# Two spectral and two dense layers on one core: rows loaded in quarters, one step of an order moved, fewer products with zeros at the seams

## The chip, the cores and the metric

The kernel runs on one core of a Trainium2 chip. The metric is the device time of one execution, in microseconds (us); lower is better. The profile is one execution of the same program, recorded instruction by instruction; its times count from the first instruction.

## The reference

The input x is a matrix of S = 2048 tokens by D = 1024 features, in bf16. Four layers follow one another, each with a residual and a layer norm in front of it:

```python
x = x + A(layernorm(x), A_w_r, A_w_i)      # spectral
x = x + B(layernorm(x), B_w1, B_b1, B_w2)  # dense
x = x + A(layernorm(x), A_w_r, A_w_i)
x = x + B(layernorm(x), B_w1, B_b1, B_w2)
```

A is a filter in the frequency domain: a real two-dimensional FFT over tokens and features, a product with the complex filter w_r + i w_i (2048 by 513), and the inverse transform. B is a feed-forward block: h = x w1 + b1 with 3584 hidden features, the activation Mish(h) = h tanh(softplus(h)), and a product with w2 back to 1024 features. A and B have the same weights in both of their layers.

## The kernel before

**Scheduling.** All instructions are written out in Python in one fixed order for each engine: TensorE (PE), VectorE (DVE), ScalarE (ACT), GpSimd (POOL) and SyncE (SP, which only issues DMAs here). Waits on semaphores are derived from which buffers an instruction reads and writes. There is no planner: the order in the text is the order on each engine. A DMA is issued by SP, ACT or POOL, in that engine's order, and the first two each have a queue of their own.

**Spectral layer (layer_A).** The FFTs are products with tables of sines and cosines.

- `s1` (L619 to L647) transforms along the outer token index. It consists of 16 groups j of eight products of 128 columns (L634). The stationary operand is the row buffer XR, in which the token rows are laid out as 128 partitions by 128 positions n by 128 features; group j reads the positions 8j to 8j+7. In layer 0 the moving operand is a table `MN`, the transform's table multiplied with each token's layer-norm scale, made group by group in `scaled` (ACT at L609 for group 1; POOL at L615 for 2, 4, 9, 10, 11 and 13; DVE at L615 for the others). Each group's result is copied out of PSUM by ACT (L640) or DVE (L642). In layer 1 the rows are already normalised and MN isn't needed. Eight PSUM banks make four pairs; one group fills one pair. In layer 0, s1 has three of them, because a fourth holds the scales.
- `s2` (L741) is the transform along features, `s3` (L786 to L789) the inner transform along tokens, followed by the product with the filter on DVE (L800 to L807); `i1` (L842) and `i2` (L872, L904) are the inverses. These four run over eight groups g with two halves each, in an order that is written out by hand in `order_A` (L1009): each number is stage, group and half, with 2 for s2, 3 for s3, 4 for i1 and 5 for i2. So 221 is the second half of s2 for group 2, and 400 the first half of i1 for group 0. Every step takes the next pair of banks in turn. The result of an s2 step is copied by ACT (L776) or DVE (L778), of s3 by ACT (L798), of i1 by ACT (L858) and of i2 by ACT (L916) or DVE (L914).
- In layer 0, `filter_bins` (L1032 to L1048) brings the filter into the order of the transform beside this, with four small products, two copies on DVE (L1043) and two on ACT (L1047) for each group.
- `u_turn` writes each group's result of i2 to a scratch tensor in HBM and reads it back with tokens and features exchanged. For the last group, ACT writes it in two halves, and four reads follow, two from ACT's queue and two from SP's (`u_last`, L948).

**The start (prologue).** SP issues, in this order: x in twelve pieces (a thirteenth comes from ACT), two small tables, the rows XR from x in packets of 256 bytes, then the tables FD and JT, the filter's rows for the first two groups, and more tables. A group of s1 waits for the part of the rows that it reads (`self.r_xr[j // 4]`).

**The seam between a spectral and a dense layer.** After the last step of order_A, TensorE has nothing real to do until the last group has been written to HBM and read back. In the text it goes on like this (L996 to L998):

```python
        self.spin(4, 0)
        self.residual_first()
        self.hold(11 if li else 16, 7)
```

`spin` makes four products of 512 columns whose result isn't used. `residual_first` puts the residual of the first 512 tokens into all eight banks. `hold` (L656) adds products with a stationary operand of zeros to bank 7, where they change nothing; they keep TensorE busy. Then the dense layer starts with `i4` (L1071), the last inverse transform. Its first 32 products wait for the first of the four reads; two more products with zeros and the next 32 follow. Its results are copied by `out_first` (L1082), normalised and turned, and the first products of the dense layer (L1220) follow.

**Dense layer (layer_B).** Products with w1 (L1220, L1260) and w2 (L1359), arranged with sums and differences of blocks so that seven block products do the work of eight. It isn't touched by the change.

Of the kernel before, what the change touches and what calls it, by code (L numbers as in the profile page):

```python
# [180 lines left out]
class KB:  # L181
# [200 lines left out]
    def prologue(self):  # L382
        sp = self.sp
        self.op(self.pool, lambda e: e.memset(self.EPS[:], 1e-5), writes=[self.r_eps, self.r_warm])
        xt = self.x[0].rearrange("(t p) d -> p t d", p=P)

        for a, b in ((10, 11), (0, 1), (1, 2), (11, 12), (2, 3), (3, 4), (12, 13), (4, 6), (13, 14), (6, 8), (14, 15), (8, 10), (15, 16)):
            self.dma(self.act if a == 10 else sp, self.XS[:, a:b, :], xt[:, a:b, :], f"x{a}", writes=self.r_xs[a:b])
        self.warm(ACT.Sqrt)
        small = {}  # L390
        def load_small(name, n, d):
            b = self.alloc(name, self.o[name], [n], d)
            self.dma(sp, b.ap, self.con[name], name.lower(), writes=[b.res])
            small[name] = b
        load_small("M0", P, BF)
        load_small("IDF", P, F32)
        self.M0, self.IDF = small["M0"], small["IDF"]

        self.XR = self.alloc("XR", self.o["XR"], [P, P])
        self.r_xr = []  # L400
        xv = self.x[0].rearrange("(n2 n1) (h l) -> h n2 n1 l", n2=16, l=P)
        for q, n in ((0, 2), (2, 1), (3, 1)):
            r = Res(f"xr{q}")
            for h in range(8):
                s = slice(32 * q, 32 * (q + n))
                self.dma(sp, self.XR.ap[h:P:8, s, :], xv[h][:, s, :], f"xr{q}", parts=[r])
            self.r_xr += [r] * n
        self.dma(sp, self.FD[:], self.con["FD"], "fd", writes=[self.r_fd])
        load_small("JT", 4 * P, BF)
        self.JT, self.r_jt = small["JT"].ap, small["JT"].res  # L410
        self.w1_next = 0
# [299 lines left out]
    def layer_A(self, li):  # L711
# [283 lines left out]
                u_turn(g, h)  # L995
        self.spin(4, 0)  # L996
        self.residual_first()
        self.hold(11 if li else 16, 7)  # L998
        if li == 0:
            self.op(self.pool, lambda e: e.tensor_copy(self.B1[:], self.B1h[:]), reads=[self.r_b1h], writes=[self.r_b1])  # L1000
        self.w1_buf = [self.alloc(f"W1_{i}", (self.ob["WS"] + i * 4096, 140 * K)[i > 4], [8, 256]) for i in range(4 if li else 6)]
# [3 lines left out]
    @staticmethod  # L1005
    def order_A():


        order = ("200 201 210 211 300 301 220 310 400 221 311 401 230 320 410 500 231 321 411 501 330 331 420 510 240 511 421 241 "  # L1009
                 "250 251 340 341 520 350 430 260 521 431 440 261 351 441 530 531 360 361 270 450 451 271 540 541 550 551 460 370 "  # L1010
                 "461 371 560 561 470 471 570 571")
        return [tuple(map(int, w)) for w in order.split()]
# [800 lines left out]
```

## Time and profile before

| | |
|---|---|
| Time, median of 3 runs | 928.98 us (928.76 to 930.48) |
| Span of the profiled execution | 923.2 us |
| TensorE busy | 877.7 us, 95% |
| DVE, ACT, POOL busy | 623.4, 435.0, 147.7 us |
| Granted TensorE clock, mean | 1.000 |
| Spectral layer 0, from the first product of s1 to the last of i2 | 24.0 to 102.2 us |
| Spectral layer 1, the same | 481.1 to 550.7 us |
| Products with zeros (L656), both seams | 31, of 379 ns each by the profile |

Matmuls are pipelined: the profile gives 379 ns to one of 512 columns, but such products start 0.216 us apart. So the time that a run of them takes is read from their starts. In the timeline a line is start, duration, engine, line of the kernel, operation, out<-in and count; in brackets stands the idle time of the engine before it and what ended it. In the chain of work that ended last, each piece is start, duration and the engine and line that held the end back.

### The profile page before, as it was taken

The page shows a single profiled execution, that of the slowest core. Times are in us where ns is not written, and L with a number is a line of the kernel's source. Part 1 is how long each engine was busy: PE and PEld are TensorE (multiplying, and loading weights), DVE is VectorE, ACT ScalarE, POOL GpSimd, SP SyncE. Part 2 cuts the span into 40 slices and gives each one's busy share as a digit, 9 for nine tenths or more (in the row PEclk, how much of TensorE's full clock was granted, in tenths as well). Part 3 has the DMA queues.
Part 4 walks back from the last instruction along what each step waited for, and adds up shares of the span by engine and source line. Part 5 has one row for each costly group of instructions (what it writes and reads, how often), then busy time and mean ns, then how long its engine had stood idle before and what let it go on. Part 6 is the DMA issues. An engine that isn't in the chain of part 4 may idle for free.

```text
span 923.2 us, 13610 instructions
## 1 busy us (share of the span) xinstructions
PE 877.7 (95%) x5503; PEld 471.1 (51%) x5503; DVE 623.4 (68%) x995; ACT 435.0 (47%) x645; POOL 147.7 (16%) x170
## 2 busy tenths in 40 slices
PE   0899889999999999999998998999999999999998
PEld 0677576444444444444456766754444444444443
DVE  7798468686889667568767765676747655554463
ACT  7898485456203485420018966757540025552000
POOL 0732004960004651010121200000000000000000
PEclk9999999999999999999999999999999999999999
DMA  9979861575786388364723786345166645732432
GB/s 279 284 249 287 219 194 67 210 266 139 262 281 239 131 317 298 121 233 143 281 92 114 221 217 161 137 175 184 23 197 189 204 148 180 269 121 86 173 129 102
DMA packets 153502, 175.98 MB, mean 191 GB/s; under 512 B 75000, under 2 KB 132568, under 8 KB 153320
## 3 DMA queue, kind: packets, MB, share of 16 engines
q1 hardware_dynamic: 140256, 130.32, 45.9%
q0 software_dynamic: 10032, 42.90, 12.5%
q10 hardware_dynamic: 3152, 1.90, 0.7%
q8 instruction: 43, 0.70, 0.3%
q14 instruction: 19, 0.16, 0.0%
HBM read 130.78 MB, written 40.89 MB: 186 GB/s over the span
## 4 chain that ended last, share of the span: by engine, by line
PE 88%; DVE 6%; ACT 3%; SPq 2%; DMA 1%; issue 0%; DVEq 0%
PE PS L1359 37%; PE PS L1260 30%; PE PS L1220 6%; PE PS L741 3%; PE PS L842 2%; PE PS L872 2%; SPq L251 2%; PE PS L1071 2%; PE PS L634 1%; PE PS L651 1%; ACT ARENA L640 1%; PE PS L1181 1%; PE PS L904 1%; PE PS L1060 1%; ACT ARENA L451 1%; PE PS L656 1%
## 5 line engine op out<-in xcount | busy, mean ns | idle before, releaser
L1359 PE MATMUL PS<-ARENA 128*128 128x512 bf16 x1568 | 340.1, 379 | 0.0
L1260 PE MATMUL PS<-ARENA 128*128 128x512 bf16 (+1 forms) x1288 | 280.4, 379 | 0.8 <-DVE ARENA L1265 0.8
L1359 PEld LDWEIGHTS PS<-ARENA 128*128 128x128 bf16 x1568 | 153.3, 98 | 184.5
L1265 DVE TENSOR_TENSOR ARENA<-PS,ARENA 128x512 f32<-128x512 f32 x230 | 157.1, 691 | 100.2 <-PE PS L1260 92.4
L1260 PEld LDWEIGHTS PS<-ARENA 128*128 128x128 bf16 x1288 | 125.3, 98 | 153.3 <-DVE ARENA L1265 3.6
L1270 ACT ACTIVATE ARENA<-ARENA,B 128x512 bf16<-128x512 f32 x138 | 98.8, 721 | 69.1 <-DVE ARENA L1265 63.8
L573 ACT ACTIVATE ARENA<-PS 128x512 f32<-128x512 f32 (+3 forms) x86 | 61.6, 726 | 110.6 <-PE PS L1260 92.5
L1153 POOL TENSOR_TENSOR ARENA<-ARENA 128x512 bf16<-128x512 bf16 x56 | 71.5, 1278 | 74.3 <-DVE ARENA L522 61.1
L451 ACT ACTIVATE ARENA<-XS 128x1024 bf16<-128x1024 bf16 x60 | 63.2, 1053 | 36.6 <-DVE XS L1410 33.0
L1220 PE MATMUL PS<-ARENA 128*128 128x256 bf16 (+1 forms) x528 | 73.4, 295 | 3.4 <-DVE ARENA L1186 1.9
L1384 DVE TENSOR_TENSOR ARENA<-ARENA 128x3584 bf16<-128x3584 bf16 x32 | 63.9, 2017 | 0.0
L1410 DVE TENSOR_TENSOR XS<-PS,ARENA 128x512 bf16<-128x512 f32 x52 | 35.7, 689 | 39.0 <-PE PS L1359 38.7
L1220 PEld LDWEIGHTS PS<-ARENA 128*128 128x128 bf16 x528 | 50.3, 98 | 22.3 <-DVE ARENA L1186 3.3
L1402 DVE TENSOR_TENSOR ARENA<-PS,ARENA 128x512 f32<-128x512 f32 x48 | 32.9, 688 | 28.0 <-PE PS L1359 27.6
L1224 ACT ACTIVATE ARENA<-PS,B 128x256 bf16<-128x256 f32 (+1 forms) x66 | 33.0, 515 | 29.0 <-PE PS L1220 28.8
L1270 ACT ACTIVATE ARENA<-PS,B 128x512 bf16<-128x512 f32 x46 | 31.5, 685 | 18.4 <-PE PS L1260 18.4
L1398 DVE TENSOR_TENSOR ARENA<-ARENA,XS 128x512 f32<-128x512 f32 x52 | 36.8, 731 | 0.5
L442 ACT ACTIVATE RS<-MV,EPS 128x1 f32<-128x1 f32 (+2 forms) x11 | 3.3, 296 | 71.5 <-DVE MV L564 70.1
L741 PE MATMUL PS<-FD,ARENA 128*128 128x256 bf16 (+1 forms) x256 | 31.4, 271 | 2.5 <-ACT ARENA L640 2.5
L842 PE MATMUL PS<-ARENA 128*128 128x256 bf16 x256 | 32.6, 273 | 1.0 <-DVE ARENA L807 0.6
L798 ACT ACTIVATE ARENA<-PS 128x1024 bf16<-128x1024 f32 x30 | 30.4, 1046 | 5.0 <-PE PS L789 5.0
L1235 DVE TENSOR_TENSOR ARENA<-ARENA 128x2048 f16<-128x2048 bf16 x16 | 25.3, 1583 | 9.0 <-PE PS L1220 8.7
(102 smaller groups left out, 811.4 us busy)
## 6 DMA issues: line engine op xcount, KB each, us to landing
ARENA<-in_B_w_dram SPq DMA_DIRECT2D x30, 896.0 KB, 6.7
ARENA<-w1s_scratch SPq DMA_DIRECT2D x28, 896.0 KB, 4.7
ARENA<-w2s_scratch SPq DMA_DIRECT2D x24, 896.0 KB, 6.6
w1s_scratch<-ARENA POOLq DMA_DIRECT2D x14, 896.0 KB, 4.6
ARENA<-in_B_w_dram SPq DMA_DIRECT2D x24, 512.0 KB, 4.3
u_scratch<-ARENA SPq DMA_DIRECT2D x14, 512.0 KB, 4.9
ARENA<-u_scratch SPq DMA_DIRECT2D x14, 512.0 KB, 6.0
w2s_scratch<-ARENA POOLq DMA_DIRECT2D x8, 896.0 KB, 4.1
```

Of the source, the lines that this page charges most:

```text
L451: self.op(act, lambda e, i=i, f=f: e.activation(junk.ap, x, f, accum_out=sums[:, i:i + 1]), reads=[self.r_xs[j]], writes=[junk.res], parts ...
L573: fn = (lambda e: e.activation(dst, src, ACT.Copy)) if scale is None else \
L741: fns.append(lambda e: e.matmul(dst, at(r), FD[:, t:t + n], start=start, stop=stop))
L842: fns.append(lambda e, c=c, part=part: e.matmul(ps[:, c * 256:(c + 1) * 256], yk.ap[:, part, c * P:(c + 1) * P], t[:, (128, 0)[part]:(384, ...
L1153: self.op(self.pool, lambda e, dst=A(dst), x=A(x), y=A(y), op=op: e.tensor_tensor(dst, x, y, op), reads=[b.res] + list(after), writes=[b.rs])
L1220: fns.append(lambda e, db=db, bank=bank, fl=fl: e.matmul(PS[:, bank, 0:w], wb.ap[:, db, fl * P:(fl + 1) * P], x.ap[:, db, tok], start=(db ...
L1260: self.group([lambda e, db=db: e.matmul(PS[:, bank, :], A[:, db, :], mov[:, db, :], start=(start and db == 0), stop=(db == 3), skip_group_ ...
L1265: self.op(dve, lambda e: e.tensor_tensor(dst.ap, PS[:, bank, :], x.ap, ALU.add), reads=[self.r_bank[bank], x.res], writes=[dst.res])
L1270: self.op(act, lambda e: e.activation(at, src, ACT.Mish, bias=self.B1[:, ft:ft + 1]), reads=[res, self.r_b1], writes=[ra])
L1359: self.group([lambda e, i=i, k=k, b=PB[n][k].ap: e.matmul(PS[:, bank, :], ap[:, i, t * P:(t + 1) * P], b[:, i - 7 * k, :], start=(start an ...
L1384: self.op(dve, lambda e: e.tensor_tensor(ap[dst][:, f, :], ap[x][:, f, :], ap[y][:, f, :], op), reads=part(x, k) + part(y, k), writes=part ...
L1398: self.op(dve, lambda e: e.tensor_tensor(a[t], a[t], x, ALU.add), reads=[rx], writes=[r[t]])
```

## The change

Three edits. The rows XR are loaded in four quarters of the positions n, with eight DMAs of 128 KB each and a semaphore of its own for each quarter, instead of a half with eight DMAs of 256 KB and then two quarters. They stay on SP's queue. The first four groups of s1 then depend on the first quarter only.

In order_A, the second half of s2 for group 2 (221) comes before the first half of i1 for group 0 (400), not after it. This holds for both spectral layers.

At the seams, hold issues 12 products with zeros instead of 16 after layer 0, and 5 instead of 11 after layer 1, so that the first real products are behind fewer of them.

```diff
-        for q, n in ((0, 2), (2, 1), (3, 1)):
+        for q in range(4):
             r = Res(f"xr{q}")
             for h in range(8):
-                s = slice(32 * q, 32 * (q + n))
+                s = slice(32 * q, 32 * q + 32)
                 self.dma(sp, self.XR.ap[h:P:8, s, :], xv[h][:, s, :], f"xr{q}", parts=[r])
-            self.r_xr += [r] * n
+            self.r_xr.append(r)
...
-        self.hold(11 if li else 16, 7)
+        self.hold(5 if li else 12, 7)
...
-        order = ("200 201 210 211 300 301 220 310 400 221 311 401 230 320 410 500 231 321 411 501 330 331 420 510 240 511 421 241 "
+        order = ("200 201 210 211 300 301 220 310 221 400 311 401 230 320 410 500 231 321 411 501 330 331 420 510 240 511 421 241 "
```

## The prediction

> **What bounds the kernel now.** I read the page first (busy shares, then the chain that ended last), then the chain in order of time, then the timeline around the three places that the diff touches, and last the DMA landings there.
>
> ```profile
> PE 877.7 (95%) x5503; PEld 471.1 (51%) x5503; DVE 623.4 (68%) x995; ACT 435.0 (47%) x645; POOL 147.7 (16%) x170
> PE 88%; DVE 6%; ACT 3%; SPq 2%; DMA 1%; issue 0%; DVEq 0%
> ```
>
> TensorE carries 88% of the chain. The two dense layers, nearly all of that, are not touched. So the change can win only where the chain leaves TensorE: at the start, in the two spectral layers, and at the two seams. The start, in the chain:
>
> ```profile
> 18.67 5.26 DMA ARENA<-in_A_x_dram
> 23.97 6.14 PE PS L634 x56
> 30.14 1.95 ACT ARENA L640 x2
> ...
> 36.99 1.03 ACT ARENA L640
> 38.02 0.09 issue
> 38.11 1.69 PE PS L741 x16
> 39.80 0.45 PE PS L1032 x4
> 40.26 1.76 PE PS L741 x16
> 42.02 0.02 issue
> 42.04 1.22 DVE ARENA L778
> ```
>
> The first products wait until 23.97 for the last DMA of the first half of the rows. Seven groups of eight follow at 110 ns a product (6.14/56; the later ones run at about 56 ns). Then ACT's copies out of PSUM set the pace, then DVE from 42.04 until 58.41.
>
> Layer 1's spectral part, TensorE alone in the timeline, has one hole:
>
> ```profile
> 497.53 0.38 PE L789 MATMUL PS<-ARENA 128*128 128x512 bf16 x1
> 498.55 1.05 PE L842 MATMUL PS<-ARENA 128*128 128x256 bf16 x8 [0.64 <-DVE ARENA L807]
> 499.43 1.04 PE L741 MATMUL PS<-FD,ARENA 128*128 128x256 bf16 x8
> ```
>
> These are starts. 512-column products start 0.216 us apart elsewhere, so between 310 and 400 (L842), which waits for DVE, 1.02 - 0.22 = 0.80 us are lost. From 498.55 on TensorE starts products without a hole until 542.99, so time saved there stays saved.
>
> The seams, in the timeline:
>
> ```profile
> 110.10 0.81 PE L656 MATMUL PS<-BD,ARENA 128*128 128x512 bf16 x3
> 110.89 0.20 PEld L1071 LDWEIGHTS PS<-MT,ARENA 128*128 128x128 bf16 x5 [0.47 <-issue]
> ...
> 557.13 1.24 PE L656 MATMUL PS<-BD,ARENA 128*128 128x512 bf16 x5
> 558.04 0.35 PEld L1071 LDWEIGHTS PS<-MT,ARENA 128*128 128x128 bf16 x5 [0.16 <-issue]
> 558.21 0.26 PE L1071 MATMUL PS<-MT,ARENA 128*128 128x32 bf16 x4
> ```
>
> L656 are the products with zeros, L1071 the first real ones behind them. The read-back they also need, by the answer on the DMA-issuing line: in layer 0 issued at 107.51, landed 3.2 us later, 110.7; in layer 1 issued at 553.82, landed 4.1 us later, 557.9. At both seams the last zeros and the data end within 0.3 us of each other.
>
> [...] from 14 to 31 us, all packets under 512 B, 217 GB/s; from 38 to 42, larger ones, 386 GB/s. So the rows are bound by packets, and cutting them otherwise leaves their total alone. [...] FD, JT and the filter rows, all queued behind the rows, land in order from 36.9. [...] Here no drop is recorded in 116.40 to 119.80, with TensorE busy for 1.64 of 3.40 us:
>
> ```profile
> 116.40:119.80 3.40, 1.64 (x28) 1.32 (x26) 2.73 (x7) 3.09 (x5) 0.00 (x0) 1.00 1.11 302
> ```
>
> **Part 1, rows in quarters.** Removed: 8 DMAs of 256 KB; added: 16 of 128 KB; same bytes, packets and queue. Such a DMA now takes 0.63 us to issue plus 0.04 between, and they land about 0.6 us apart (the 256 KB ones 1.24). The first quarter therefore lands near 15 + 7 x 0.6 = 19 us instead of the half at 23.9. It is no longer last: MN0 is ready at 22.77 (DVE), MN1 at 24.13 (eight ACT instructions). So group 0 starts at about 22.83, but group 1 at 24.19 where it was at 24.80. From there groups follow at 0.855 us, and ACT's copy of group 6, at 30.14 now, comes at 29.53: 0.6 us sooner. Behind it the ACT chain (0.905 us a copy) keeps the lead to group 12, which wants the last quarter. That lands at 33.46 now (issue 30.42 + 3.0) and is needed at 33.4 then: a tie. The last group waits for DVE's MN15: group 10's copy 32.2 to 33.4, two scalings to 35.65, products, ACT copy 36.4 to 37.4, instead of 38.02. So s2 (L741) starts 0.6 us sooner, FD having landed at 36.9.
>
> Not all of that survives. L1032 needs the filter rows behind the rows in the ring; they land at 32.87 + 6.3 = 39.2. TensorE reaches L1032 at 39.0 then and waits until 39.28, where it started at 39.64: 0.36 us kept. This carries to L778 at 42.04 and along DVE, which has no hole over 0.04 us until 58.4. Both ends: if the smaller DMAs are issue-bound (32 x 0.67 us[...]) the rows end up to 1.2 us later, and the part costs up to 0.8; if the filter rows come sooner, it gives 0.6. I take **0.36**. No wait is added; only filter and tables are queued behind.
>
> **Part 2, the order.** 221, eight L741 products at 0.109 us, moves from behind 400 to before it. In layer 1 it fills the hole: 221 from 497.75 to 498.62, then 400 at 498.62 (DVE ready at 498.50), 311 at 499.49, 401 at 500.36, where DVE's L807 for it ends only at 500.49; so 401 starts at 500.55 instead of 501.17. Gain **0.62**, at most 0.80, at least 0 if ACT takes it: ACT now copies 221 ahead of 400, so the copy of 400 goes from 499.63 to 499.88. The copies of 311 and 320 still come 0.66 us sooner, because ACT's idle 0.51 before 499.63 is filled. DVE, which waits for 320's copy until 505.27, gets it at 504.6. In layer 0 the same hole is 0.23 us and DVE is the bound from 42.04 to 58.4, its order untouched: nothing.
>
> **Part 3, fewer zeros.** Four fewer in layer 0 take 0.86 us out of TensorE's stream, six in layer 1 1.29. In layer 0 the gap after the last L656 is already the read-back's (landing 110.7, first weights 110.89): 0. In layer 1 the first weights went in at 558.04, 0.1 after the landing, and the first product had to wait for the zeros until 558.21; it could have started at 558.07: **0.14**. The two zeros and the second read-back behind it (issued 554.46, landed 559.0) allow that. TensorE will stand about 0.9 and 1.2 us idle instead of multiplying zeros. The tail beyond, out_first and the statistics, just follows.
>
> Sum: 0.36 + 0.62 + 0 + 0.14 = 1.12 us, all on the chain; 928.98 - 1.12 = 927.9.
>
> **Rivals.** *A, the zeros are the bound.* Write and read-back take 4.4 + 3.2 us in layer 0 and 2.2 + 4.1 in layer 1 in this one execution, so a landing moves by a microsecond. Should the data usually be there early, 0.86 + 1.29 = 2.15 come free instead of 0.14: 928.98 - 0.98 - 2.15 = 925.9. For it: the near ties. Against: both ties go to the data here.
> *B, the clock falls at the seams.* [...] Against it: the 48% window that kept its clock. The rows' tail coming 1.2 us later would give no more than 929.1.
> *C, the start is hidden anyway.* The filter rows slip by the 0.36 that part 1 keeps: 928.98 - 0.62 - 0.14 = 928.2.
>
> **How the numbers follow.** My forecast 0.47, A 0.28, C 0.14, B 0.11. 0.2% is 1.86 us: A falls outside on the fast side (its partial forms too, where one seam alone gains; some of my own case, with 0.62 from part 1 and 0.80 from part 2, comes near), B on the slow side. Faster 0.35, same 0.52, slower 0.13. The range runs from just short of A's full form, 925.6, to 930.2, which takes in a late rows' tail with no gain from the order, or a clock lost at one seam.
>
> **What would show it.** Right: the first L634 near 22.8, bounded by L615 and not by a DMA; L778 about 0.4 us sooner than 42.04; no hole before L842 in layer 1, and the stretch from its first L741 to its last L872 0.6 us shorter; before the first L1071 a gap of 0.9 to 1.2 us ended by the read-back. Wrong: the last rows landing after 34; that stretch unchanged; L1071 following the zeros at once, or the read-back landing much sooner than 3 us after its issue; any granted clock under 1.00.

## The result, and the profile after

| | before | after |
|---|---|---|
| Time, median of 6 runs | 928.87 us (927.86 to 930.48) | 934.07 us (931.79 to 936.91) |
| Ratio | | 1.0057, 95% interval 1.0035 to 1.008 |
| Span of the profiled execution | 923.2 us | 931.0 us |
| Granted TensorE clock, mean | 1.000 | 0.996 |

The change makes the kernel slower by 0.57%, 5.2 us. The prediction, 927.9, said slightly faster, and its range ended at 930.2.

From the page of the kernel after, the span, part 1, one queue of part 3 and the shares of part 4:

```profile
span 931.0 us, 13598 instructions
PE 876.7 (94%) x5493; PEld 470.8 (51%) x5493; DVE 623.7 (67%) x995; ACT 435.3 (47%) x645; POOL 147.6 (16%) x170
q8 instruction: 43, 0.70, 0.3%
PE 84%; DVE 5%; SPq 4%; DMA 4%; ACT 3%; issue 1%; ACTq 0%; DVEq 0%
```

TensorE did the same work, less 10 recorded products. But its share of the chain of waits fell from 88 to 84%, and SPq (SyncE issuing DMAs) and DMA together rose from 3 to 8%. So TensorE waits more, and what it waits for is loads. The line of q8 will matter further down.

Where the time comes from is read from the same starting points in both traces (times of start in us; the last column is what was added since the row above):

| | before | after | later by | added |
|---|---|---|---|---|
| first L778 on DVE (end of s1's wait, layer 0) | 42.04 | 43.90 | 1.86 | +1.86 |
| last L904 of layer 0 | 101.98 | 103.78 | 1.80 | -0.06 |
| first L1071 (i4, layer 0) | 110.92 | 112.80 | 1.88 | +0.08 |
| spin of 31 products ahead of layer 1 (L651) | 474.02 | 476.03 | 2.01 | +0.13 |
| first L634 of layer 1 | 481.09 | 487.00 | 5.91 | +3.90 |
| first L741 of layer 1 | 491.00 | 498.17 | 7.17 | +1.26 |
| first L842 of layer 1 | 498.55 | 505.79 | 7.24 | +0.07 |
| last L904 of layer 1 | 550.52 | 557.08 | 6.56 | -0.68 |
| first L1071, layer 1 | 558.21 | 565.47 | 7.26 | +0.70 |
| first L1220 behind it | 567.14 | 574.99 | 7.85 | +0.59 |
| end | 923.18 | 931.04 | 7.86 | +0.01 |

These are single executions, so the sum, 7.9, is not the 5.2 of the medians; the rows show the places. The profiled execution of the kernel before is a quick one besides: it took 925.04 us, less than any of the six timed ones. Part of that is luck at the start: its L778 at 42.04 is the earliest of the eight traces, here and below, of kernels that load the rows as before (42.04 to 43.75, mean 43.03), so the +1.86 of the first row is more than the change usually costs there. The largest row is one that the diff doesn't touch: TensorE's wait for the rows of layer 1, at 481.

**The start.** The chain of waits of the kernel after, from 14 us on (start, duration, what held the end back):

```profile
14.70 0.63 SPq L251
15.32 0.04 issue
15.37 0.63 SPq L251
...
32.15 0.63 SPq L251
32.78 0.04 issue
...
34.61 6.84 DMA ARENA<-in_A_w_i_dram
...
43.90 1.23 DVE ARENA L778
```

Each line of 0.63 is SyncE issuing one of the 32 row DMAs, and they follow one another with nothing between but 0.04. The last starts at 32.15 (30.42 before) and lands at 35.13 (33.46 before): 2.98 and 3.04 us after the issue. In the changed kernel this distance is about 3 us from the sixth of the 32 DMAs on, so the rows wait for SyncE and not for the DMA engines. In the kernel before the distance shrinks, from over 7 us for the first DMAs to 3.04 for the last: there the engines were the bound for most of the time. The line of SyncE's queue in the DMA view, before from 14 to 31 us and after from 16 to 33 (packets, MB, and the sum of the packets' times as a share of 16 engines, which overlap takes over 100%), says the same; the mean rate is 217 and 196 GB/s:

```profile
q1 hardware_dynamic: 14730, 3.69, 125.9%
```

```profile
q1 hardware_dynamic: 13392, 3.33, 86.7%
```

Everything behind them in the queue is as late: the filter rows are the last link before DVE's 43.90. On TensorE, in the timeline of the kernel after:

```profile
22.67 1.01 PE L634 MATMUL PS<-ARENA 128*128 128x128 bf16 x8 [1.68 <-DVE ARENA L615]
31.66 0.62 PE L634 MATMUL PS<-ARENA 128*128 128x128 bf16 x8 [0.22 <-ACT ARENA L640]
35.17 1.51 PE L634 MATMUL PS<-ARENA 128*128 128x128 bf16 x24 [2.89 <-DMA ARENA<-in_A_x_dram]
39.05 1.69 PE L741 MATMUL PS<-FD,ARENA 128*128 128x256 bf16 x16 [1.45 <-DMA FD<-c_fd]
```

The early start came as meant (22.67, released by DVE's scaling and not by a DMA; 23.97 before). It is lost at the fourth quarter: group 12 waits 2.89 us for its rows. Over all traces the last row lands at 33.46 to 35.87 with the rows as before (eight traces, mean 34.5), and at 34.62 to 36.04 with 32 DMAs from SyncE (five traces, mean 35.2); L778 follows at 43.0 and 44.2 on average. In three of these five, but in one of the eight, the wait ahead of the last rows is followed by half the clock (at 34 to 36 us).

**The rows of layer 1.** GpSimd stores each normalised block of rows to xn_scratch, and SyncE reads it back in order and then brings the last rows over directly. The timeline of the kernel after, around the spin of 31 products (L651):

```profile
473.66 0.89 POOL L251 DMA_DIRECT2D xn_scratch<-ARENA  x1 [2.23 <-DVE ARENA L1398]
476.03 6.85 PE L651 MATMUL PS<-BD 128*128 128x512 bf16 x31
480.33 3.81 SPq L251 DMA_DIRECT2D ARENA<-ARENA  x6
487.00 1.25 PE L634 MATMUL PS<-M,ARENA 128*128 128x128 bf16 x15 [4.12 <-DMA ARENA<-ARENA]
```

The same of the kernel before:

```profile
471.65 0.89 POOL L251 DMA_DIRECT2D xn_scratch<-ARENA  x1 [2.23 <-DVE ARENA L1398]
474.02 6.85 PE L651 MATMUL PS<-BD 128*128 128x512 bf16 x31
477.09 3.74 SPq L251 DMA_DIRECT2D ARENA<-ARENA  x6
481.09 1.95 PE L634 MATMUL PS<-M,ARENA 128*128 128x128 bf16 x32 [0.21 <-issue]
```

The store stands 2.37 us ahead of the spin in both. But SyncE's direct copies start 4.30 us behind the spin's start after, 3.07 before. They stand behind the read-back of that store, and it landed late. By the answer on the DMA-issuing line for that store alone, before and after:

```profile
DMA to landing us min/median/max: 2.8/2.8/2.8
```

```profile
DMA to landing us min/median/max: 6.0/6.0/6.0
```

**The clock.** The windows of the kernel after (start:end, length, busy us of each engine, then the granted clock, DMA share and GB/s):

```profile
484.18:487.59 3.41, 0.59 (x11) 0.62 (x12) 0.00 (x0) 0.00 (x0) 0.00 (x0) 1.00 0.06 13
487.60:491.01 3.41, 3.41 (x36) 3.41 (x34) 2.50 (x3) 1.93 (x2) 0.00 (x0) 0.50 0.00 0
...
562.69:566.10 3.41, 1.58 (x31) 0.88 (x30) 0.00 (x0) 0.00 (x0) 0.00 (x0) 1.00 0.99 150
566.10:569.52 3.42, 3.42 (x105) 2.87 (x102) 2.04 (x5) 1.67 (x3) 0.00 (x0) 0.50 0.50 142
```

The granted clock is 1.00 here but for two stretches at 0.50. These last 3.41 and 3.42 us and start 78.50 us apart, 23 times 3.413, so the text cuts the time into windows of 3.413 us that lie on this grid. TensorE is busy for 0.59 us of the first window, and the next one has half the clock: that is the +1.26 of s1 in the table. The third window is the end of the second seam, now with fewer zeros in it; the half clock in the fourth is the +0.59.

**The seams.** Timeline of the kernel after, first and second seam:

```profile
109.06 2.79 PE L656 MATMUL PS<-BD,ARENA 128*128 128x512 bf16 x12
112.80 0.95 PE L1071 MATMUL PS<-MT,ARENA 128*128 128x32 bf16 x32 [0.94 <-DMA ARENA<-u_scratch]
...
562.36 1.28 PE L656 MATMUL PS<-BD,ARENA 128*128 128x512 bf16 x5
565.47 0.98 PE L1071 MATMUL PS<-MT,ARENA 128*128 128x32 bf16 x32 [1.83 <-DMA ARENA<-u_scratch]
```

Both gaps are ended by the read-back, as forecast. From the last L904 to the first L1071 it took 9.02 us in layer 0 (8.94 before) and 8.39 in layer 1 (7.69 before).

### The profile page after: what moved, and what is told of

The parts are those of the page before. It is cut to its first block, busy times and chain, and to the rows that moved or that the text cites. A ratio compares the mean times of both kernels' runs of the same rounds, so it can differ in the third digit from the quotient of the medians.

```text
span 931.0 us, 13598 instructions
## 1 busy us (share of the span) xinstructions
PE 876.7 (94%) x5493; PEld 470.8 (51%) x5493; DVE 623.7 (67%) x995; ACT 435.3 (47%) x645; POOL 147.6 (16%) x170
## 4 chain that ended last, share of the span: by engine, by line
PE 84%; DVE 5%; SPq 4%; DMA 4%; ACT 3%; issue 1%; ACTq 0%; DVEq 0%
PE PS L1359 36%; PE PS L1260 29%; PE PS L1220 6%; SPq L251 4%; PE PS L741 2%; PE PS L842 2%; PE PS L872 2%; PE PS L1071 2%; DMA ARENA<-u_scratch 1%; PE PS L1181 1%; DMA ARENA<-in_A_w_i_dram 1%; DMA u_scratch<-ARENA 1%; ACT ARENA L451 1%; ACT ARENA L640 1%; ACT ARENA L573 1%
## 5 line engine op out<-in xcount | busy, mean ns | idle before, releaser
L1220 PE MATMUL PS<-ARENA 128*128 128x256 bf16 (+1 forms) x528 | 73.4, 295 | 3.4 <-DVE ARENA L1186 1.9
L1220 PEld LDWEIGHTS PS<-ARENA 128*128 128x128 bf16 x528 | 50.2, 98 | 22.3 <-DVE ARENA L1186 3.3
L741 PE MATMUL PS<-FD,ARENA 128*128 128x256 bf16 (+1 forms) x256 | 31.4, 271 | 2.7 <-DMA FD<-c_fd 1.4
L842 PE MATMUL PS<-ARENA 128*128 128x256 bf16 x256 | 32.6, 273 | 0.3 <-DVE ARENA L829 0.3
```

The costliest lines, as they stand in the source:

```text
L741: fns.append(lambda e: e.matmul(dst, at(r), FD[:, t:t + n], start=start, stop=stop))
L842: fns.append(lambda e, c=c, part=part: e.matmul(ps[:, c * 256:(c + 1) * 256], yk.ap[:, part, c * P:(c + 1) * P], t[:, (128, 0)[part]:(384, ...
L1220: fns.append(lambda e, db=db, bank=bank, fl=fl: e.matmul(PS[:, bank, 0:w], wb.ap[:, db, fl * P:(fl + 1) * P], x.ap[:, db, tok], start=(db ...
```

## The experiments

Ratios are to the kernel before on the same chip, with 95% intervals. Its medians were 927.31 us for the first four kernels, 928.37 for the next four, 927.76 for the last four.

**The rows in quarters alone.**

```diff
-        for q, n in ((0, 2), (2, 1), (3, 1)):
+        for q in range(4):
...
-                s = slice(32 * q, 32 * (q + n))
+                s = slice(32 * q, 32 * q + 32)
...
-            self.r_xr += [r] * n
+            self.r_xr.append(r)
```

> The kernel before with the rows in four quarters alone. Theory, the rows are bound by issuing: 32 DMAs at 0.67 us each put the last row 1.7 us later (35.1 instead of 33.5), FD, JT and the filter rows behind them follow, and L778 comes near 43.9 instead of 42.04: about 1.8 us slower, 930.7. Rival, the prediction: packets bind, the start gains 0.36 us, 928.5.

Measured: 1.0029 (1.0019 to 1.0039), 930.19 us. This part costs 2.7 us by itself. Its profiled execution, the shortest of its 16, has L778 at 42.63, 0.59 later than the profile of before, but within what other executions with the rows as before show. TensorE is idle around 31 to 35 us; the granted clock is 0.998. So at the start a good execution loses nothing, and the loss comes in the others.

**The order alone.**

```diff
-        order = ("200 201 210 211 300 301 220 310 400 221 311 401 230 320 410 500 231 321 411 501 330 331 420 510 240 511 421 241 "
+        order = ("200 201 210 211 300 301 220 310 221 400 311 401 230 320 410 500 231 321 411 501 330 331 420 510 240 511 421 241 "
```

> The kernel before with 221 ahead of 400 alone. Theory, and the prediction too: the hole before the first L842 of layer 1 is filled and nothing else moves, 0.6 us faster, 928.3. Rival: ACT's other order takes it back, no change. If the layer-1 spectral stretch is 0.6 us shorter in the trace, the first holds whatever the time says.

Measured: 0.9993 (0.9982 to 1.0004), 927.29 us; the interval takes in no change, so the trace has to show the gain. The timeline of this kernel in layer 1:

```profile
498.99 1.04 PE L741 MATMUL PS<-FD,ARENA 128*128 128x256 bf16 x8
499.86 1.04 PE L842 MATMUL PS<-ARENA 128*128 128x256 bf16 x8
500.73 0.38 PE L786 MATMUL PS<-ARENA 128*128 128x512 bf16 x1
...
501.38 0.38 PE L789 MATMUL PS<-ARENA 128*128 128x512 bf16 x1
501.79 1.05 PE L842 MATMUL PS<-ARENA 128*128 128x256 bf16 x8
```

221 (first line) now fills the hole ahead of 400 (second line). Of the 0.80 us lost there, a wait of 0.41 - 0.22 = 0.19 us comes back before 401 (last line). So 0.61 us stay. From the first L741 to the last L904 of layer 1 it takes 58.91 us, where before took 59.52 (0.61 less; the same to 0.01 in every kernel with the new order, and unchanged in the ones without).

**The zeros alone, 12 and 5.**

```diff
-        self.hold(11 if li else 16, 7)
+        self.hold(5 if li else 12, 7)
```

> The kernel before with 12 and 5 products with zeros alone. Theory, the clock:[...] with what the start costs left out the remainder of the loss is here: up to 3.9 us slower, 931 to 932.8, and granted clocks under 1.000. Rival, the prediction: 0.14 us faster, clock 1.000.

Measured: 1.0039 (1.0025 to 1.0053), 931.35 us. The loss isn't at the seams: from the last L904 to the first L1071 the two seams take 8.82 and 7.79 us (before: 8.94, 7.69). It is at the rows of layer 1, 350 us later: the first L634 comes 9.67 us after the spin's start, where before has 7.07, and s1 then takes 1.24 us longer at half the clock.

**Rows and order, without the zeros.** The two edits above.

> The changed kernel with 16 and 11 products with zeros put back (rows in quarters and the new order). If the zeros carry the loss that the rows don't, 1.2 us slower than the kernel before, 930.1. If the zeros do nothing, as slow as the changed kernel, 934.

Measured: 1.0000 (0.9986 to 1.0013), 927.87 us. In its trace the wait for layer 1's rows is as before (7.02 us). It came out better than the product of its parts, 1.0029 x 0.9993 = 1.0022; the interval ends at 1.0013, and no run explains the rest.

**Fewer zeros still: 4 and 1.**

```diff
-        self.hold(11 if li else 16, 7)
+        self.hold(1 if li else 4, 7)
```

> The kernel before with 4 and 1 products with zeros, so 12 and 10 fewer where the change took 4 and 6: the suspected cost is amplified. Theory, the clock: 2.8 us idle at the first seam and 2.3 at the second[...], at least 0.6 us each, and the loss is larger than that of 12 and 5 on the same chip, 1.5 to 4 us. Rival, the loss measured with 12 and 5 came from slow DMAs in those executions and not from the zeros: under 1 us slower.

Measured: 0.9976 (0.9961 to 0.9991), 927.48 us: faster than before, although it has fewer zeros than the changed kernel. So the number of zeros has no simple cost. From the last L904 to the first L1071: 7.40 us in both layers. First L634 of layer 1: 7.90 after the spin's start.

**The changed kernel again.**

> The changed kernel once more beside its parts on one chip. If parts add up: rows +2.7, order -0.6, zeros +3.6 as measured, 5.7 us slower. If the zeros' 3.6 was the execution's DMAs: near 2 us slower.

Measured: 1.0051 (1.0038 to 1.0064), 933.38 us. First L634 of layer 1 10.03 us after the spin's start, followed by s1 with 1.26 us lost.

**The zeros of one seam each.**

```diff
-        self.hold(11 if li else 16, 7)
+        self.hold(5 if li else 16, 7)
```

> The kernel before with 5 products with zeros after layer 1 alone (16 stay after layer 0). Theory, the clock:[...] 0.3 to 0.9 us slower on average. Rival, the prediction: 0.14 us faster.

```diff
-        self.hold(11 if li else 16, 7)
+        self.hold(11 if li else 12, 7)
```

> The kernel before with 12 products with zeros after layer 0 alone (11 stay after layer 1). Theory, the clock: about 1.1 us idle[...], under 0.3 us slower. Prediction: no change.

Measured: 0.9989 (0.9978 to 1.0001), 927.85 us, with 5 zeros in layer 1; 1.0029 (1.0016 to 1.0042), 931.08 us, with 12 in layer 0. So four products with zeros less at 107 us cost 2.7 us, and the wait is at 481: first L634 10.69 us after the spin's start, against 7.17 with 5 zeros in layer 1.

What can four products at 107 us change at 467? The stores there share the DMA engines with the queue q8, of kind "instruction", which moves 43 packets in this program, 0.70 MB, so 16 KB each. In the DMA view of the kernel before, from 466.0 to 467.1, and of the kernel with 12 zeros in layer 0, from 467.2 to 468.8 (packets, MB, share of 16 engines):

```profile
q0 software_dynamic: 24, 0.10, 23.7%
q8 instruction: 1, 0.02, 5.3%
```

```profile
q0 software_dynamic: 68, 0.22, 36.8%
q8 instruction: 1, 0.02, 5.7%
```

q0 is GpSimd's queue with the stores. One such packet passes near each time, but not at the same point. Its start against the spin's start, and what follows, in single executions:

| zeros in layer 0 | packet of q8 | first of three stores lands after | last of three | first L634 after the spin's start |
|---|---|---|---|---|
| 16 (before) | -7.91 | 3.25 | 2.84 | 7.07 |
| 12 (alone) | -7.03 | 4.52 | 6.41 | 10.69 |
| 12 (changed kernel) | -7.02 | 4.82 | 6.01 | 10.98 |
| 4 and 1 | -5.42 | 2.83 | 2.83 | 7.90 |

The ten other traces fall into the same groups. With 16 zeros, or with 12 and four products put back, the packet is at -8.29 to -7.86 and the first L634 at 7.02 to 7.56; with 12 zeros, at -7.16 to -7.02 and 9.67 to 10.98; with 4, at -5.45 and -5.42, and 7.44 and 7.90.

Four products less move the packet 0.88 us later (4 x 0.216 = 0.86), twelve less 2.49 (12 x 0.216 = 2.59). So the packet goes with TensorE's count of instructions in these traces, and it is read here as a fetch of TensorE's own program; no run shows that directly. With 16 zeros the packet starts 0.76 us after the issue of the first store (at -8.67), with 12 zeros 1.65 us after it, in the thick of its packets. The first store then lands 4.5 to 4.8 us after its issue instead of 3.25, SyncE's read of it goes out later and runs beside the third store instead of the second. SyncE waits in its order for that third store, and behind it stand the direct copies of the last rows.

**The packet put back.** If that is the cause, four other products ahead of it must undo the loss, wherever they stand. Here layer 0's seam keeps its 12 zeros, and four products whose result isn't used go in behind the four groups of i4, where TensorE waits for ACT and DVE (0.74 to 0.93 us at a time in the kernel before).

```diff
-        self.hold(11 if li else 16, 7)
+        self.hold(11 if li else 12, 7)
...
-        rests = [staged_rest(0, 10)]
+        self.spin(4, 0) if not li else None; rests = [staged_rest(0, 10)]
```

> The kernel before with 12 products with zeros after layer 0, and four idle products (spin) put into the hole of TensorE behind the first i4 groups of the same seam (about 115 us, 0.95 us wide). Theory, instruction fetch: the four products removed moved the 16 KB fetch of TensorE's instructions near 466 us by 0.86 us, onto the store of a normalised row block; with the count restored it falls 7.9 us before the spin of 31 again, the store takes 3.3 us, the first product of layer 1 comes 7.0 to 7.4 us after the spin begins and not 9.7 to 11, and the time is that of the kernel before within 0.1%. Rival, fewer zeros at the seam slow it by themselves: as slow as 12 alone, +0.3%.

Measured: 0.9995 (0.9981 to 1.0009), 927.10 us. The timeline of this kernel at the rows of layer 1:

```profile
471.69 0.89 POOL L251 DMA_DIRECT2D xn_scratch<-ARENA  x1 [2.23 <-DVE ARENA L1398]
474.06 6.85 PE L651 MATMUL PS<-BD 128*128 128x512 bf16 x30
477.13 3.73 SPq L251 DMA_DIRECT2D ARENA<-ARENA  x6
481.08 2.99 PE L634 MATMUL PS<-M,ARENA 128*128 128x128 bf16 x48 [0.17 <-issue]
```

The four lines stand as in the kernel before, to 0.04 us. The packet is at -7.86 again, the last store lands after 2.83. The seam with 12 zeros lost nothing either: from the last L904 to the first L1071 it took 7.90 us. So the count of zeros as such, and the clock at the seam, fall as causes of this part's loss.

**The same put back in the changed kernel.** The added line is the same.

```diff
+        self.spin(4, 0) if not li else None; rests = [staged_rest(0, 10)]
```

> The changed kernel with the same four products in the same hole. Theory, instruction fetch: 3 us or more of the 4.7 us loss go, what stays is the rows less the order, about +0.2%. Rival: still +0.5%.

Measured: 1.0004 (0.9992 to 1.0015), 928.42 us, against 1.0051 without the line. First L634 of layer 1 7.31 us after the spin's start. The late rows are still in this kernel (L778 at 46.62, with three windows at half the clock from 34.47 to 44.71); the parts that gain about make up for them: 1.0029 for the rows x 0.9993 for the order x 0.9989 for layer 1's zeros x 0.9995 for the packet put back is 1.0006. The same product with 1.0029 for the packet shifted is 1.0040, of the 1.0051 and 1.0057 that the changed kernel has.

**The order with 4 and 1 zeros.**

```diff
-        self.hold(11 if li else 16, 7)
+        self.hold(1 if li else 4, 7)
...
-        order = ("200 201 210 211 300 301 220 310 400 221 311 401 230 320 410 500 231 321 411 501 330 331 420 510 240 511 421 241 "
+        order = ("200 201 210 211 300 301 220 310 221 400 311 401 230 320 410 500 231 321 411 501 330 331 420 510 240 511 421 241 "
```

> The kernel before with the new order and 4 and 1 products with zeros. If the two parts measured alone add up (0.9976 and 0.9993): ratio 0.997, 2.9 us faster. If the gain of 4 and 1 hung on where the fetch fell and the new order upsets nothing of that, the same.

Measured: 0.9990 (0.9973 to 1.0007), 925.89 us: no better than 4 and 1 zeros alone.

**The quarters without the queue.** The rows in quarters and the new order, and a quarter of the row DMAs issued by GpSimd, which is idle there, once x has landed. SyncE issues 24 as before, and 8 go beside them.

```diff
-                self.dma(sp, self.XR.ap[h:P:8, s, :], xv[h][:, s, :], f"xr{q}", parts=[r])
+                late = h > 5
+                self.dma(self.pool if late else sp, self.XR.ap[h:P:8, s, :], xv[h][:, s, :], f"xr{q}{late}",
+                         reads=self.r_xs[15:16] if late else (), parts=[r])
```

> The kernel before with the new order and the rows in quarters, of which GpSimd issues 8 of 32 DMAs (the last two of each quarter's eight) once x is in, and SP 24. Theory, issue-bound: with 24 issues on SP the last row lands near 33.4 again and the early start is kept, L778 at 41.7 to 42.2; with the order's 0.6 about 1 us faster than before. Rival: the packets of two queues share the DMA engines[...], the first group starts after 24 and nothing is gained by the rows.

Measured: 0.9968 (0.9951 to 0.9984), 924.45 us: faster than the kernel before, and by the ratios faster than the changed one. Its timeline (lines below the edit are numbered 2 higher, so L636 is the product of s1, L780 DVE's copy of s2):

```profile
10.87 19.12 SPq L251 DMA_DIRECT2D ARENA<-in_A_x_dram  x21
...
14.76 5.12 POOL L251 DMA_DIRECT2D ARENA<-in_A_x_dram  x8 [13.90 <-DMA XS<-in_A_x_dram]
...
22.72 1.01 PE L636 MATMUL PS<-ARENA 128*128 128x128 bf16 x8 [1.63 <-issue]
...
32.84 1.76 PE L636 MATMUL PS<-ARENA 128*128 128x128 bf16 x24 [0.39 <-DVE ARENA L644]
...
40.82 1.23 DVE L780 CAST ARENA<-PS 128x1024 bf16<-128x1024 f32 x1 [1.50 <-PE PS L743]
```

SyncE is done with the rows at 30, the fourth quarter is there at 32.79, and TensorE's wait of 2.89 us is 0.39. The early start is kept and DVE begins at 40.82, 1.22 us sooner than before and 3.08 sooner than in the changed kernel. With the order's 0.61 that is 1.8 us. Against the mean of the traces with the rows as before, 43.03, DVE begins 2.2 us sooner, which makes 2.8; the timed gain is 3.0, with an interval of 1.5 to 4.5.

This run shares out the issuing, but that isn't all it does. From 17.4 to 25.5 us the two queues moved 251 GB/s together, and GpSimd's has far larger packets (0.94 MB in 345, against 1.09 MB in 4407):

```profile
q1 hardware_dynamic: 4407, 1.09, 73.4%
q0 software_dynamic: 345, 0.94, 44.7%
```

How much of the gain is SyncE's time and how much the larger packets, no run separates. That the changed kernel waits for the issuing rests on its own trace, on the fixed 3 us.

**Windows at half the clock, counted.** The stretches at half the clock in the profile of the changed kernel last 3.41 us, and in that of the changed kernel with the packet put back three follow one another from 34.47 to 44.71, 3.413 us each. One such window is 1.71 us off the mean. So the granted clock of each timed run gives an estimate of how many it had: (1 - clock) x span / 1.71. The clock is given to three places, which leaves about a third of a window open.

| | windows a run, mean | median at 0 | at 1 | at 2 |
|---|---|---|---|---|
| before, with the first four | 0.7 | 926.95 | 928.30 | 930.29 |
| before, with the next four | 0.8 | 927.72 | 928.69 | 930.69 |
| before, with the last four | 0.6 | 926.71 | 928.26 | 930.17 |
| changed kernel (both times) | 4.0, 3.8 | | | 932.90, 931.61 |
| rows alone | 2.4 | | 928.93 | 930.20 |
| order alone | 0.8 | 926.32 | 927.64 | 929.01 |
| 12 and 5 zeros | 1.5 | | 930.98 | 931.40 |
| rows and order | 1.6 | | 926.83 | 928.53 |
| 5 zeros, layer 1 | 1.1 | 926.93 | 927.44 | 929.41 |
| 12 zeros, layer 0 | 1.5 | 930.34 | 930.31 | 931.66 |
| 4 and 1 zeros | 1.6 | 924.99 | 926.27 | 928.16 |
| order, 4 and 1 zeros | 2.1 | 924.30 | 925.14 | 926.14 |
| packet put back, 12 zeros | 0.5 | 926.93 | 928.95 | 930.38 |
| packet put back, changed kernel | 2.4 | 926.19 | 928.07 | 928.63 |
| rows partly from GpSimd, order | 0.6 | 923.67 | 926.18 | 926.47 |

In the kernel before, one such window goes with 1.0 to 1.6 us, and two with 3.0 to 3.5. The changed kernel has three more of them a run. They are cause and symptom at once, since in the traces the clock fell behind waits of TensorE, so this table is a reading and not an experiment. Three things show in it. The rows alone are slower than before by 0.6 us at one window and not at all at two, but have 1.7 windows more a run: most of their 2.7 us goes with the clock. The order gains 0.6 to 1.3 us at equal counts. And 4 and 1 zeros gain 2.4 to 2.7 us at equal counts but have one window more a run; with the order as well, 2.4 to 4.0 us, and 1.5 windows more. So with fewer zeros a run gains time and pays part of it back in clock.

## Why the prediction was wrong

**Part 1 failed, at the step "the rows are bound by packets, and cutting them otherwise leaves their total alone".** That was a fair reading of the kernel before, whose DMA engines were full (125.9% by the sum above, against 86.7% after). But in DMAs of 128 KB from one queue the rows are bound by their issue: 0.67 us each, landing 3.0 us after the last. The text had this case as its far end, "up to 1.2 us later", and took the near one, for a gain of 0.36. In the two profiled executions the rows end 1.67 us later and L778 1.86; on average over the traces it is about 0.7 and 1.2. Alone the part costs 2.7 us. By the count of windows most of that goes with the clock, which the part had put at nothing: the wait for the fourth quarter leaves a thin window, and half the clock follows it in three of five traces. The step that looked harmless was "lands at 33.46 now (issue 30.42 + 3.0) [...] a tie": it kept the issue time of a queue with 24 DMAs for one with 32. The two numbers to set against each other were on the page: 0.67 us to issue and about 0.6 to land. The first half of the part was right: start at 22.67 (forecast 22.83), released by DVE. With a quarter of the DMAs on GpSimd's queue the start gives 1.22 us, more than forecast.

**Part 2 was right.** Forecast 0.62, measured 0.61 in the traces; the ratio, 0.9993, fits it but its interval reaches past 1.

**Part 3 failed at a step that wasn't there.** At the seam of layer 0 the forecast of nothing is about what the two traces show (8.94 and 9.02 us), and the gap before L1071 is the read-back's, as forecast. But "the tail beyond [...] just follows" left out that products with zeros are instructions too. With four fewer of them a packet of q8 came 0.88 us later against the work at the stores of layer 1's rows, 1.65 us behind the issue of the first instead of 0.76, and that store landed after 4.5 us instead of 3.25. That costs 2.7 us (1.0029), and putting four products elsewhere takes it back (0.9995; in the changed kernel from 1.0051 to 1.0004). That the packet is TensorE's program and that it delays the store is read from where it falls in the traces; the runs show that the count of products ahead decides. In layer 1 the forecast was 0.14: timed 0.9989 (0.9978 to 1.0001), with single traces that show the seam longer.

**Rival A, "the zeros are the bound", fell at the seam of layer 0,** although the seam does get shorter with fewer zeros. In six traces with 16 zeros there the way from L904 to L1071 is 8.87 to 9.11 us, in six with 12 it is 7.90 to 9.02, in two with 4 it is 7.40 and 7.83. But in all fourteen the first L1071 starts 0.24 to 0.40 us after the read-back has landed, so the data end the wait each time. What differs is the write ahead of the read-back. By the answer on the DMA-issuing line for the second half of the last group's write, in the kernel before and in the one with the packet put back:

```profile
DMA to landing us min/median/max: 4.4/4.4/4.4
```

```profile
DMA to landing us min/median/max: 2.0/2.0/2.0
```

In eight traces, the six with 16 zeros and two with 12, it lands after 4.2 to 4.5 us, and a packet of q8 starts 2.0 to 2.5 us after the last L904, about a microsecond into it. In the other six that packet comes 8.3 to 9.6 us after L904, and the write lands after 2.0 to 2.8. So the packet in the way is the likely reason here too; no run moves this packet alone, and why 12 zeros have it in either place stays open. In layer 1 the zeros ended the wait in two traces of fourteen, by about 0.15 us in the kernel before, as forecast, and by 0.27 with 12 zeros in layer 0.

**Rival B, "the clock falls at the seams", was given too little, 0.11.** The evidence against it was one stretch, 48% busy, that kept its clock. It was cut at an arbitrary place and not along the windows of 3.413 us, and a busy share of that size says little: in the changed kernel a window with TensorE busy for 1.58 of 3.41 us, 46%, stood ahead of a half clock at the second seam. What a fall of the clock costs was the author's estimate, which the trace of before, at 1.000, doesn't show. In the changed kernel one window at 0.50 goes with 1.26 us more in layer 1's s1, and one with 0.59 behind the second seam. At the second seam fewer zeros aren't needed for it: with the rows alone and all 11 zeros the clock halved at 569.27, behind a window with 1.61 us busy. B's place was half wrong: more was lost in layer 1's s1, behind the idle time that the late rows made, than at the seam.

**Rival C,** a start that stays hidden, fell: against the profile of before the start came out on both sides of it, 1.86 us later in the changed kernel and 1.22 sooner with GpSimd's queue.

Time 934.07 lies beyond 930.2 because three losses came together: late rows in layer 0 (1.0029 alone), the shifted packet (1.0029 alone), and the windows at half the clock that both bring. The range held one of them at a time.

**What stays open.** Why rows and order together cost less than their parts, and 12 and 5 zeros together more than theirs (1.0039, against 1.0029 x 0.9989 = 1.0018). Whether 5 zeros in layer 1 gain anything: the interval ends at 1.0001, and the trace shows no gain. And how the version with GpSimd does with other counts of zeros, or with SyncE's time and the size of packets told apart: neither was tried.

## What to carry to other kernels

Before cutting DMAs into smaller ones, set their issue time against the time between their landings; where the first is larger, as here with 0.67 us against about 0.6, the count of DMAs on a queue is a cost, and another engine's queue is worth a trial. Products that only fill time still do something: with fewer of them most of these kernels had more windows at half the clock (with the rows as before, 1.1 to 2.1 a run against 0.6 to 0.8; but 0.5 with the packet put back), and four fewer moved a packet of q8 by 0.88 us some 360 us later, so after changing their number look at every tight DMA chain behind, not only at the seam itself. And a loss far from the edit is tested by restoring what the edit shifted at another place.

## What the hardware showed that was not expected

- The queue q8, of kind "instruction", moved 43 packets of 16 KB through the DMA engines in each of the fourteen traces, in the kernel before mostly 25 to 29 us apart in the dense layers. With 4 and 12 products less the one at the rows of layer 1 came 0.88 and 2.49 us later, so they are read here as TensorE's program. The first of the three stores of 256 KB landed after 2.8 us where no such packet came while it ran, after 3.2 to 3.7 where one started 0.4 to 0.8 us behind its issue, and after 4.0 to 4.8 where one started 1.5 to 1.7 us behind it; the packet itself then took 1.2 to 1.6 us.
- The granted clock halved behind windows with some work in them, and the busy time that the profile gives draws no edge: in the changed kernel it halved behind 1.58 us busy of 3.41 (from 562.69) and not behind 1.54 (from 33.61), and in the kernel with the new order and 4 and 1 zeros it halved behind 1.92 (from 109.80).
- SyncE's time to issue was the bound of the rows in the changed kernel: 0.67 us a DMA from the sixth of 32 on, where those of the kernel before landed about 0.6 us apart. With a quarter of the issues on GpSimd SyncE was done at 30.0 us instead of 32.8, and the last landing went from 35.13 to 32.79, though with larger packets on that queue as well (2.7 KB on average, against 250 bytes).
- The same read-back of 128 KB at the second seam took 4.1 us to land in the profile of the kernel before and 4.8 in that of the changed one, so that one trace can't tell which of two near ties is the bound.
